# Value products of the later attention runs on 64x64 quarters, in two PSUM banks, with a VectorE add

## The chip, the cores and the metric

The kernel runs on one core of one Trainium2 chip. The metric is device time in microseconds (us). The core has a matrix engine (TensorE, PE in the profile; PEld is its weight load), VectorE (DVE), ScalarE (ACT), GpSimd (POOL) and SyncE (SP), which start from their own instruction lists and wait for each other by semaphores, and DMA queues. Matrix products leave their sums in PSUM, a memory of eight banks of 128 partitions by 512 float32 values.

## The reference, cut to what matters

Three stages follow one another: attention with a window of 128 keys, a feed-forward layer with ReLU, and a gated layer that mixes over the sequence.

```python
scores = scale * np.matmul(q, k.transpose(0, 1, 3, 2))      # B, H, S, D = 4, 8, 576, 64
...
mask = (rel >= 0) & (rel < window)                           # window = 128
scores = np.where(mask, scores + bias[None], -1000000000.0)
...
attn = attn / (np.sum(attn, axis=-1, keepdims=True) + 1e-09)
return np.matmul(attn, v).astype(np.float32)
...
ch = np.maximum(xn @ w_ch1, 0.0) @ w_ch2                     # 512 -> 2048 -> 512, on layer-normed rows
return (x + ch).astype(np.float32)
...
h = x @ w_in                                                 # 512 -> 1024, then a tanh-GELU
u, v = (h[..., :d_ff // 2], h[..., d_ff // 2:])
...
v_s = np.einsum('ts,bsd->btd', w_sg, v_n) + b_sg[None, :, None]
return (x + (u * v_s) @ w_out).astype(np.float32)
```

## The kernel before

Two phases follow each other on the core. `phase1` does attention and the feed-forward layer, the second phase the gated layer.

Attention is cut into 40 runs, numbered n = 0 to 39. Runs 0 to 31 hold two blocks of 128 queries of one pair of heads; their order is batch, half of the sequence (`i0` = 0 or 2), pair of heads, so that four first-half runs (`i0` = 0) and four second-half runs (`i0` = 2) alternate. Runs 32 to 39 are "tails": the last 64 queries of two pairs of heads. A block of queries is a unit; there are 72.

For each run PE makes the scores (`quarters`, L465, L451 for the tails), on tiles of 64x64 of its array. The other engines turn scores into probabilities `t`; PE transposes `t` (`transposed`, L593) into the PSUM bank `tps`; DVE, ACT and POOL copy the transposes, masked, into `m` (L551, L554, L474); PE multiplies `m` by the values (`values`, L633) into columns 0 to 255 of the bank `ob`, and ACT copies that into `x` (L588, L585 for the tails). Partitions 0 to 63 of `ob` are one head, 64 to 127 the other, and columns are queries. A value product takes up to 128 keys by 64 columns of the array (a form 128x64); its passes are three, over the key blocks `i0` - 1, `i0` and `i0` + 1 with 128, 256 and 128 query columns, where a first-half run has only the last two. A tail takes 128 keys and then 64 keys for each pair.

From `KB` = 13 on, PE does attention in bursts (`burst`): the scores of run n + 1, the values of run n - 1 and the transposes of run n, one after the other, without anything between. There are 27 bursts, and the values of run 39 follow alone.

Between the bursts PE does the feed-forward products: L796 (first matrix, into `ps_h`) and L807 (second, into `acc`), each as three products of split operands, twelve matmuls of 128x256 to a half-step. ACT makes the ReLU (L735), DVE the rest of the split (`hl`, L737), and DVE and POOL add the result to `x` (L746, L750). Per group of rows a mean is needed before: POOL sums `x` over its four parts (`sum`, L659 and L661) and PE multiplies that by a matrix of ones (L664); DVE subtracts it (`xc`, L668).

The order on each engine is set at build time by a planner (`Sched`): pieces of work are `Op`s with an engine, an assumed duration, a due time and what they need, and the planner lists them. The durations assumed for bursts (`dur` in `burst`) and for the other pieces shape that order only. Ahead of the first burst the planner fills PE's gaps with matmuls on `ob[:, 256:512]` whose result nobody reads (L853).

Of the kernel before, what the change touches and what calls it, by code (L numbers as in the profile page):

```python
# [11 lines left out]
ACTF = mybir.ActivationFunctionType  # L12
ALU = mybir.AluOpType
# [51 lines left out]
KB = 13  # L65
# [167 lines left out]
def phase1(tc, nc, a, x2d, cst, p2):  # L233
# [37 lines left out]
    ps_s = tc.alloc_tile_pool(name="ps_s", bufs=1, space=PSUM)  # L271
    both = ps_s.tile([128, 2, 2, 256], F32, name="s")
    xt = {}

# [211 lines left out]
    def unit(e):  # L486
# [43 lines left out]
        e.t = t  # L530
        tp = tps[:, un % 2]
        if n >= KB:
# [48 lines left out]
        if sl:  # L581
            xt[x] = xp.tile([128, 4, 256], F32, tag="x", name="x")
        x, p = xt[x], s.p
        if tail:
            act.activation(out=x[:, p:p + 2, s.b * 64:s.b * 64 + 64],  # L585
                           in_=s.O[:, 0:128].rearrange("p (y r) -> p y r", y=2), func=ACTF.Copy)
        else:
            act.activation(out=x[:, p, :], in_=s.O, func=ACTF.Copy)  # L588
        yield Op(None, 0, 0, token=("ev", n))

    def transposed(e):
        for h in range(2):
            pe.transpose(tps[:, e.un % 2, h], e.t[:, h], ident)  # L593

    def burst(s):
# [5 lines left out]
        if after:  # L601
            nd += [("lq", n + 1), ("lk", n + 1)]
            sl.append(("s", 1, ("cp", n + 1)))
        dur = 430 + 140 * len(s.units) + (530 if runs[n - 1].tail else 820 if runs[n - 1].i0 else 600)
        if after:
# [7 lines left out]
        for z in [("A1", n + 1), ("C", n - 1)] + [("T", e.un) for e in s.units]:  # L613
            sched.done[z] = sched.free["PE"] + HOPP

    def values(s):

        s.O = ob[:, 0:256]
        if s.tail:
# [219 lines left out]
    def warm():  # L839

        z = np_.tile([128, 256], F32, tag="rstd", name="zero", bufs=3).bitcast(BF16)
        dve.memset(z, 0.0)
        ps = ps_a.tile([128, 2, 256], F32, tag="a0", name="warm").rearrange("p a b -> p (a b)")
        for n in range(NWARM):
            pe.matmul(ps, z[:, 0:128], z, start=True, stop=True)
        sched.free["PE"] = PE0
        yield Op(None, 0, 0, need=["al"])
        while ("w", 23) not in sched.done:
            yield Op("PE", 213, 10 ** 9)
            if ("w", 23) in sched.done:  # L850
                return
            for x in range(2):
                pe.matmul(ob[:, 256:512], dist[:, 0], dist[:, 0:2], start=True, stop=True, skip_group_check=True)  # L853
            yield Op(None, FILL, 10 ** 9)
# [459 lines left out]
```

## Time and profile before

| | |
|---|---|
| runs of the kernel before | 744.79, 746.72 and 746.82 us, median 746.72 |
| the profiled execution | 746.11 us, of which the span of the trace is 744.4 us |
| PE busy | 728.3 us, 98% of the span |
| DVE, ACT, POOL busy | 454.8, 309.6 and 245.5 us |
| granted clock of TensorE, as a mean | 0.995 of full speed |

The span is the time from the first to the last instruction in the trace; 1.7 us of the execution lie around it. Busy time says how long an engine worked on something; an engine that shows idle time gives with it what released it. The chain that ended last follows the work back from the end, at each step to what released it. A window table gives busy times by stretch, so that a stretch in which PE has no gap is told from one in which it waits.

### The profile page before, as it was taken

How to read it: one execution, taken by the hardware profiler on the slowest of the kernel's cores; microseconds unless marked ns; L12 is line 12 of the kernel's file. 1: busy time of each engine (PE TensorE's matmuls, PEld its weight loads, DVE VectorE, ACT ScalarE, POOL GpSimd, SP SyncE). 2: the span in 40 equal slices, each digit the busy share in tenths (PEclk: the TensorE clock that was granted, in tenths of full speed). 3: DMA queues.
4: the chain of work that ended last, by engine and by line, in shares of the span. 5: the costliest groups of instructions: out<-in, count | busy, mean ns of one | idle time of the engine just before them, and what ended most of it. 6: DMA issues, size and time to landing. Idle time of an engine off the chain costs nothing.

```text
span 744.4 us, 16207 instructions
## 1 busy us (share of the span) xinstructions
PE 728.3 (98%) x6442; PEld 687.8 (92%) x6442; DVE 454.8 (61%) x1173; ACT 309.6 (42%) x794; POOL 245.5 (33%) x295
## 2 busy tenths in 40 slices
PE   6989999999999999999999999999999999999998
PEld 3568999999999999999998999999999999999997
DVE  6899989888562642633533344938585646647632
ACT  5887664444342422422423433323454334243410
POOL 1444250243421411411412222314738307326220
PEclk9999999999999999999999999999999999999999
DMA  9564532032221110111111223423340150160002
GB/s 309 155 206 140 188 103 65 27 92 93 75 87 30 54 51 23 48 58 41 43 48 45 72 76 119 130 98 102 110 128 1 48 158 1 49 207 2 1 33 96
DMA packets 51627, 63.44 MB, mean 85 GB/s; under 512 B 10336, under 2 KB 38880, under 8 KB 51552
## 3 DMA queue, kind: packets, MB, share of 16 engines
q1 hardware_dynamic: 51552, 62.41, 26.7%
q8 instruction: 51, 0.84, 0.5%
q14 instruction: 24, 0.20, 0.1%
HBM read 52.96 MB, written 9.44 MB: 84 GB/s over the span
## 4 chain that ended last, share of the span: by engine, by line
PE 86%; DVE 7%; ACT 4%; POOL 1%; issue 1%; DMA 0%; DVEq 0%; ACTq 0%; SPq 0%
PE acc L807 25%; PE ps_h L796 24%; PE ps_s L1157 8%; PE ps_o L1184 7%; PE ps_v L1061 5%; PE ps_u L1141 5%; PE o L633 4%; PE tps L593 3%; PE s L465 2%; ACT t L516 1%; DVE sc L94 1%; DVE sc L97 1%; ACT t L480 1%; PE s L451 1%; POOL vnl L1051 0%
## 5 line engine op out<-in xcount | busy, mean ns | idle before, releaser
L737 DVE SCALAR_TENSOR_TENSOR hl<-ps_h,hh 128x512 fp32r<-128x512 f32 x72 | 49.7, 690 | 115.0 <-ACT hh L735 114.6
L807 PE MATMUL acc<-hh,w2h 128*128 128x256 f32 x576 | 93.8, 285 | 0.0
L796 PE MATMUL ps_h<-xh,w1h 128*128 128x256 f32 x576 | 91.8, 281 | 0.0
L735 ACT ACTIVATE hh<-ps_h 128x512 fp32r<-128x512 f32 x72 | 42.9, 595 | 114.8 <-PE ps_h L796 114.4
L796 PE MATMUL ps_h<-xh,w1l 128*128 128x256 f32 x576 | 89.8, 278 | 0.0
L796 PE MATMUL ps_h<-xl,w1h 128*128 128x256 f32 x576 | 89.8, 278 | 0.0
L807 PE MATMUL acc<-hh,w2l 128*128 128x256 f32 x576 | 89.6, 278 | 0.0
L807 PE MATMUL acc<-hl,w2h 128*128 128x256 f32 x576 | 89.5, 278 | 0.0
L474 POOL TENSOR_SCALAR_AFFINE_SELECT m<-m 128x256 f32<-128x256 f32 (+1 forms) x85 | 38.6, 455 | 146.1 <-ACT m L554 143.5
L796 PEld LDWEIGHTS ps_h<-xh,w1h 128*128 128x128 f32 x576 | 76.9, 188 | 1.1 <-issue 1.1
L807 PEld LDWEIGHTS acc<-hh,w2h 128*128 128x128 f32 x576 | 77.5, 189 | 0.4
L796 PEld LDWEIGHTS ps_h<-xh,w1l 128*128 128x128 f32 x576 | 76.9, 188 | 0.0
L796 PEld LDWEIGHTS ps_h<-xl,w1h 128*128 128x128 f32 x576 | 76.9, 188 | 0.0
L807 PEld LDWEIGHTS acc<-hh,w2l 128*128 128x128 f32 x576 | 76.8, 188 | 0.0
L807 PEld LDWEIGHTS acc<-hl,w2h 128*128 128x128 f32 x576 | 76.6, 188 | 0.0
L516 ACT ACTIVATE t<-t,sm 128x128 f32<-128x128 f32 x144 | 56.2, 392 | 23.3 <-DVE sm L510 22.8
L524 POOL TENSOR_TENSOR t<-t,sm 128x256 f32<-128x256 f32 x46 | 28.7, 625 | 63.2 <-DVE sm L520 32.9
L1051 POOL TENSOR_TENSOR gl<-gt,gh 128x576 fp32r<-128x576 f32 x16 | 23.4, 1465 | 49.2 <-ACT gh L1050 45.9
L85 ACT ACTIVATE sc<-st 128x512 f32<-128x512 f32 (+1 forms) x52 | 30.6, 600 | 21.3 <-DMA st<-in_w 6.8
L1095 ACT ACTIVATE ge<-ge 128x512 f32<-128x512 f32 (+1 forms) x34 | 22.4, 658 | 36.0 <-DVE ge L1094 36.0
L551 DVE TENSOR_TENSOR m<-tps,munf 128x256 f32<-128x256 f32 x43 | 16.9, 420 | 33.4 <-PE tps L593 32.8
L593 PE MATMUL tps<-ident,t 128*128 128x128 f32 x144 | 28.5, 299 | 8.1 <-POOL t L524 3.7
(160 smaller groups left out, 1587.4 us busy)
## 6 DMA issues: line engine op xcount, KB each, us to landing
st<-in_w SPq DMA_DIRECT2D x24, 512.0 KB, 4.3
x2d<-x SPq DMA_DIRECT2D x18, 256.0 KB, 2.0
out<-xr SPq DMA_DIRECT2D x15, 288.0 KB, 2.1
st<-in_w SPq DMA_DIRECT2D x16, 256.0 KB, 2.7
st<-in_wi SPq DMA_DIRECT2D x8, 512.0 KB, 4.0
st<-x2d SPq DMA_DIRECT2D x8, 512.0 KB, 5.0
xr<-x2d SPq DMA_DIRECT2D x8, 512.0 KB, 7.4
rq<-in_q SPq DMA_DIRECT2D x28, 128.0 KB, 2.7
```

What stands on the lines that cost most here:

```text
L85: self.nc.scalar.activation(out=self.x, in_=self.wh.bitcast(F32), func=ACTF.Abs)
L474: pool.affine_select(out=out, in_=in_, pattern=pat, compare_op=ALU.is_ge, fill=0.0, base=-1 if up else 0, channel_multiplier=1 if up else -1)
L516: act.activation(out=t[:, h], in_=t[:, h], func=ACTF.Exp, bias=st[:, h:h + 1], scale=-1.0, accum_out=sums[:, h, 0:1])
L593: pe.transpose(tps[:, e.un % 2, h], e.t[:, h], ident)
L735: act.activation(out=h, in_=ps, func=ACTF.Relu)
L737: dve.scalar_tensor_tensor(out=l, in0=ps, scalar=0.0, in1=h.bitcast(F32), op0=ALU.max, op1=ALU.subtract)
L796: pe.matmul(ps[:, half], w[:, kc, f], m[:, kc], start=kc == 0 and x == 0, stop=kc == 3 and x == 2)
L807: pe.matmul(accs[half][:, d], w[:, f, ds], m[:, k], start=fi and d == 0 and k == 0 and x == 0, stop=la and k == 1 and x == 2, skip_group_c ...
L1061: self.nc.tensor.matmul(ps[:, cs], xs[s][:, kc, c0:c0 + 128], self.wv[m][:, kc, cs], start=kc == 0 and x == 0 and z == 0, stop=kc == 3 and ...
L1141: pe.matmul(ps[:, c], wu[s][:, kc, ds], self.x[m][:, kc, c], start=kc == 0 and x == 0, stop=kc == 3 and x == 2)
L1157: pe.matmul(ps[:, c], l, r[:, c], start=n == 0, stop=n == len(mm) - 1)
L1184: pe.matmul(ps[:, c], wo[s][:, kc, ds], gated[b][m][:, kc, c], start=n == 0, stop=n == 11)
```

## The change

The runs from 12 on (`KB` - 1) take a new function `quartered`. A product of up to 128 keys by 64 columns becomes two of 64 keys by 64 columns on two different halves of the array's rows: keys 0 to 63 of each block add up in columns 0 to 255 of `ob`, keys 64 to 127 in the same columns of `tps`. The window leaves some query columns of a half without any key; those columns are left out of the product. In a second-half run the first half of the keys has 64 + 192 + 128 columns and the second half 128 + 192 + 64, where the 128-key product had 128 + 256 + 128 = 512. In a first-half run they are 320 and 256 (before 384), in a tail 256 and 128 (before 256, in four steps of 64).

ACT copies `ob` into `x` as before, and DVE then adds the sums in `tps` to `x` (new line, `dve.tensor_tensor`). In first-half runs columns 0 to 63 of the second sums are never written and the add leaves them out. Over 28 runs there are 12 adds of 128x256, 8 of 128x192 and 8 of 128x2x64. The sum on POOL, and so the mean, now needs the add.

Since both banks hold value sums in columns 0 to 255, the transposes from run 13 on go to columns 256 to 511 (`spot`): even units into `ob`, odd ones into `tps`. The planner's assumed durations follow. The filling matmuls end with the first scores of a burst. The lines of the changed program are later by 1 up to the scores (L465 is L466), by 13 at the transposes (L606) and by 39 from the values on (L796 is L835, L659 is L698); the quartered values are L650.

```diff
@@ -270,6 +270,7 @@
     ob = ps_o.tile([128, 512], F32, name="o")
     ps_s = tc.alloc_tile_pool(name="ps_s", bufs=1, space=PSUM)
     both = ps_s.tile([128, 2, 2, 256], F32, name="s")
+    pair = ob, tps.rearrange("p a b c -> p (a b c)")
     xt = {}
 
     def by(o):
@@ -528,7 +529,7 @@
                 scaled(o.eng, t[:, h], t[:, h], st[:, 6 + h:7 + h])
 
         e.t = t
-        tp = tps[:, un % 2]
+        tp = spot(e)
         if n >= KB:
             yield Op(None, 0, pri, need=[("T", un)])
         else:
@@ -581,16 +582,28 @@
         if sl:
             xt[x] = xp.tile([128, 4, 256], F32, tag="x", name="x")
         x, p = xt[x], s.p
+        y = x[:, p, :]
+        os = [z[:, 0:256] for z in pair]
         if tail:
-            act.activation(out=x[:, p:p + 2, s.b * 64:s.b * 64 + 64],
-                           in_=s.O[:, 0:128].rearrange("p (y r) -> p y r", y=2), func=ACTF.Copy)
-        else:
-            act.activation(out=x[:, p, :], in_=s.O, func=ACTF.Copy)
+            y = x[:, p:p + 2, s.b * 64:s.b * 64 + 64]
+            os = [z[:, 0:128].rearrange("p (y r) -> p y r", y=2) for z in pair]
+        act.activation(out=y, in_=os[0], func=ACTF.Copy)
+        if n >= KB - 1:
+            yield Op("DVE", 205 if tail else 340, pri + OC)
+            cut = 64 if i == 1 else 0
+            y, o = (y, os[1]) if tail else (y[:, cut:], os[1][:, cut:])
+            dve.tensor_tensor(out=y, in0=y, in1=o, op=ALU.add)
         yield Op(None, 0, 0, token=("ev", n))
+
+    def spot(e):
+
+        if e.run.n < KB:
+            return tps[:, e.un % 2]
+        return pair[e.un % 2][:, 256:512].rearrange("p (h c) -> p h c", h=2)
 
     def transposed(e):
         for h in range(2):
-            pe.transpose(tps[:, e.un % 2, h], e.t[:, h], ident)
+            pe.transpose(spot(e)[:, h], e.t[:, h], ident)
 
     def burst(s):
         n = s.n
@@ -601,7 +614,7 @@
         if after:
             nd += [("lq", n + 1), ("lk", n + 1)]
             sl.append(("s", 1, ("cp", n + 1)))
-        dur = 430 + 140 * len(s.units) + (530 if runs[n - 1].tail else 820 if runs[n - 1].i0 else 600)
+        dur = 290 + 140 * len(s.units) + (480 if runs[n - 1].tail else 640 if runs[n - 1].i0 else 530)
         if after:
             dur += 530 if after.tail else 850 if after.i0 else 700
         yield Op("PE", dur, (after or s).tau, need=nd, slots=sl)
@@ -613,8 +626,34 @@
         for z in [("A1", n + 1), ("C", n - 1)] + [("T", e.un) for e in s.units]:
             sched.done[z] = sched.free["PE"] + HOPP
 
+    def quartered(s):
+
+
+        a0, a1 = slice(0, 64), slice(64, 128)
+        if s.tail:
+            mm = [[(g, 2 * z, 3, 64 * z, 64 * z, 64) for z in range(2)] for g in (a0, a1)]
+            mm[0] += [(a0, 2 * z + 1, 4, 64 * z, 64 * z, 64) for z in range(2)]
+        else:
+            mm = [[], []]
+            if s.i0:
+                mm[0].append((a0, s.i0 - 1, s.i0 - 1, 0, 0, 64))
+                mm[1].append((a1, s.i0 - 1, s.i0 - 1, 0, 0, 128))
+            mm[0] += [(a0, s.i0, s.i0, 0, 0, 192), (a0, s.i0 + 1, s.i0 + 1, 128, 0, 128)]
+            mm[1] += [(a1, s.i0, s.i0, 64, 64, 192), (a1, s.i0 + 1, s.i0 + 1, 192, 64, 64)]
+        for x in range(len(mm[0])):
+            for g in range(2):
+                if x >= len(mm[g]):
+                    continue
+                k, j, m, oc, mc, w = mm[g][x]
+                for h in range(2):
+                    v = s.v[j // 2][k, j % 2, h, :] if s.tail else s.v[0][k, j - s.k0, h, :]
+                    pe.matmul(pair[g][64 * h:64 * h + 64, oc:oc + w], v, s.M[m][k, h, mc:mc + w], start=x == 0,
+                              stop=x == len(mm[g]) - 1, skip_group_check=True)
+
     def values(s):
 
+        if s.n >= KB - 1:
+            return quartered(s)
         s.O = ob[:, 0:256]
         if s.tail:
             mm = [(128, 2 * z, 3, 64 * z, 64 * z, 64) for z in range(2)]
@@ -845,9 +884,9 @@
             pe.matmul(ps, z[:, 0:128], z, start=True, stop=True)
         sched.free["PE"] = PE0
         yield Op(None, 0, 0, need=["al"])
-        while ("w", 23) not in sched.done:
+        while ("A1", KB) not in sched.done:
             yield Op("PE", 213, 10 ** 9)
-            if ("w", 23) in sched.done:
+            if ("A1", KB) in sched.done:
                 return
             for x in range(2):
                 pe.matmul(ob[:, 256:512], dist[:, 0], dist[:, 0:2], start=True, stop=True, skip_group_check=True)
```

On PE the change shows in the bursts. This is the one with the scores of a first-half run and the values of a second-half run (`o` is `ob`). Before:

```order
L465 MATMUL s<-rk,rq 64x192 x4
L633 MATMUL o<-m,rv 64x128 [waits DMAHW5_49]
L633 MATMUL o<-m,rv 64x128
L633 MATMUL o<-m,rv 64x256 [waits Pool_49]
L633 MATMUL o<-m,rv 64x256
L633 MATMUL o<-m,rv 64x128 [waits Pool_49]
L633 MATMUL o<-m,rv 64x128
L593 MATMUL tps<-ident,t 128x128 [waits Pool_49]
L593 MATMUL tps<-ident,t 128x128
L593 MATMUL tps<-ident,t 128x128 [waits Activation_49] x2
```

Now, on PE in the same burst:

```order
L466 MATMUL s<-rk,rq 64x192 x4
L650 MATMUL o<-m,rv 64x64 [waits DMAHW5_49]
L650 MATMUL o<-m,rv 64x64
L650 MATMUL tps<-m,rv 64x128 x2
L650 MATMUL o<-m,rv 64x192 [waits Pool_49]
L650 MATMUL o<-m,rv 64x192
L650 MATMUL tps<-m,rv 64x192 x2
L650 MATMUL o<-m,rv 64x128 [waits Pool_49]
L650 MATMUL o<-m,rv 64x128
L650 MATMUL tps<-m,rv 64x64 x2
L606 MATMUL o<-ident,t 128x128 [waits Pool_49]
L606 MATMUL o<-ident,t 128x128
```

Six value products became twelve with fewer columns in each bank, and the first two transposes go to `o`; PE waits for the same engines as before.

On DVE, behind the same burst, the copies, the mask and the softmax of the next scores follow. Before:

```order
L737 SCALAR_TENSOR_TENSOR hl<-ps_h,hh 128x512 [waits Activation_49]
L551 TENSOR_TENSOR m<-tps,munf 128x2x128 [waits PE_49]
L500 COPY_PREDICATED s<-mask,mh 128x2x128
L498 COPY_PREDICATED s<-mask,s 128x2x128 [waits DVE_49]
L510 ISA t,sm_121<-s,dist 128x128 [waits DVE_49]
```

Now, on DVE at the same place:

```order
L776 SCALAR_TENSOR_TENSOR hl<-ps_h,hh 128x512 [waits Activation_49]
L552 TENSOR_TENSOR m<-o,munf 128x2x128 [waits Activation_49]
L501 COPY_PREDICATED s<-mask,mh 128x2x128
L595 TENSOR_TENSOR x<-x,tps 128x192 [waits DMAHW3_49,DMAHW4_49,Activation_49,Pool_49]
L511 ISA t,sm_121<-s,dist 128x128 [waits DVE_49]
```

The product `m` waits for ACT (its copy out of the same bank) where it waited for PE, and the add stands ahead of the softmax.

On POOL the sum for a group's mean is the place where the add is waited for, here for the group of runs 20 to 23. Before:

```order
L659 TENSOR_TENSOR sum<-x 128x512 [waits Activation_49]
L474 AFFINE_SELECT m<-m 128x2x128 [waits Activation_49]
L661 TENSOR_TENSOR sum<-sum 128x256 [waits Pool_49]
L474 AFFINE_SELECT m<-m 128x256 [waits PE_49,Pool_49]
L524 TENSOR_TENSOR t<-t,sm_121 128x256 [waits DVE_49,PE_49,Activation_49]
```

Now, on POOL at the same place:

```order
L475 AFFINE_SELECT m<-m 128x2x128 [waits Activation_49]
L698 TENSOR_TENSOR sum<-x 128x512 [waits DVE_49]
L475 AFFINE_SELECT m<-m 128x256 [waits PE_49,Pool_49]
L700 TENSOR_TENSOR sum<-sum 128x256 [waits Pool_49]
L525 TENSOR_TENSOR t<-t,sm_121 128x256 [waits DVE_49,PE_49,Activation_49]
```

The sum waits for DVE where it waited for ACT, and one of the mask selects moved ahead of it.

## Rows read from the trace of the kernel before

**Rows 1.** Page: busy time of each engine (share of the span), then the chain's shares.

```profile
PE 728.3 (98%) x6442; PEld 687.8 (92%) x6442; DVE 454.8 (61%) x1173; ACT 309.6 (42%) x794; POOL 245.5 (33%) x295
...
PE 86%; DVE 7%; ACT 4%; POOL 1%; issue 1%; DMA 0%; DVEq 0%; ACTq 0%; SPq 0%
```

**Rows 2.** Windows: stretch, length, busy PE, PEld, DVE, ACT, POOL, granted clock, DMA share.

```profile
128.00:200.00 72.00, 72.00 (x672) 69.02 (x672) 57.42 (x159) 33.76 (x96) 27.32 (x36) 1.00 0.22 68
200.00:300.00 100.00, 100.00 (x951) 94.22 (x951) 45.26 (x151) 32.05 (x102) 22.45 (x36) 1.00 0.18 53
300.00:400.00 100.00, 100.00 (x934) 94.33 (x934) 44.86 (x152) 33.43 (x105) 22.60 (x38) 1.00 0.16 45
400.00:455.00 55.00, 55.00 (x571) 50.87 (x568) 18.47 (x67) 20.46 (x65) 15.65 (x27) 1.00 0.27 76
455.00:600.00 145.00, 144.54 (x1208) 144.25 (x1208) 96.05 (x153) 58.24 (x97) 64.04 (x51) 1.00 0.29 94
```

**Rows 3.** Timeline (start, length, xrecords), PE: burst, first-half scores, second-half values.

```profile
165.78 0.77 PE L465 MATMUL s<-rk,rq 64*64 64x64 f32 x16
166.48 1.09 PE L633 MATMUL o<-m,rv 128*64 128x128 f32 x12
167.50 0.66 PE L593 MATMUL tps<-ident,t 128*128 128x128 f32 x4
167.91 0.72 PE L807 MATMUL acc<-hh,w2h 128*128 128x256 f32 x4
```

**Rows 4.** Timeline, PE: burst with second-half scores and first-half values.

```profile
227.61 0.88 PE L465 MATMUL s<-rk,rq 64*64 64x192 f32 x16
228.42 0.87 PE L633 MATMUL o<-m,rv 128*64 128x256 f32 x8
229.23 0.66 PE L593 MATMUL tps<-ident,t 128*128 128x128 f32 x4
```

**Rows 5.** Timeline, PE: a tails' burst, and the last values, alone.

```profile
421.21 0.56 PE L451 MATMUL s<-rk,rq 64*64 64x192 f32 x8
421.70 0.83 PE L633 MATMUL o<-m,rv 128*64 128x64 f32 x16
422.46 0.44 PE L593 MATMUL tps<-ident,t 128*128 128x128 f32 x2
...
451.80 0.83 PE L633 MATMUL o<-m,rv 128*64 128x64 f32 x16
452.56 0.61 PE L807 MATMUL acc<-hh,w2h 128*128 128x256 f32 x3
```

**Rows 6.** Timeline: from a burst's transposes to a group's mean (runs 20 to 23).

```profile
297.25 0.66 PE L593 MATMUL tps<-ident,t 128*128 128x128 f32 x4
...
297.36 0.38 ACT L588 ACTIVATE x<-o 128x256 f32<-128x256 f32 x1 [2.43 <-PE o L633]
...
297.83 1.29 POOL L659 TENSOR_TENSOR sum<-x 128x512 f32<-128x512 f32 x1 [8.24 <-ACT x L588]
...
297.94 0.42 DVE L551 TENSOR_TENSOR m<-tps,munf 128x256 f32<-128x256 f32 x1 [2.29 <-PE tps L593]
...
299.07 0.60 POOL L474 TENSOR_SCALAR_AFFINE_SELECT m<-m 128x256 f32<-128x256 f32 x1
...
299.44 0.43 DVE L498 COPY_PREDICATED s<-mask,s 128x256 f32<-128x256 uint8 x1
...
299.64 0.74 POOL L661 TENSOR_TENSOR sum<-sum 128x256 f32<-128x256 f32 x1
...
301.85 0.59 PE L664 MATMUL ps_ln<-sum,ones 128*128 128x256 f32 x2
```

**Rows 7.** Timeline: where DVE frees `acc` shortly before PE writes it.

```profile
193.07 0.67 DVE L746 TENSOR_TENSOR et<-acc,rstd 128x512 f32<-128x512 f32 x1
...
194.25 0.63 PE L807 MATMUL acc<-hh,w2h 128*128 128x256 f32 x4
```

## The prediction

> **What bounds the kernel now.** I read the page's busy times and its chain first. PE is busy for 98% of the span and carries 86% of the chain, DVE 61% and 7% [rows 1]. Shares over the whole span say nothing of one stretch, so the windows come next. The change touches the time from the first burst, at 128 us, to the last values, at 452 us. In the four stretches from 128 to 455 us PE is busy for every microsecond, at the full granted clock (1.00, the 2.4 GHz level), while DVE works 57.42, 45.26, 44.86 and 18.47 us [rows 2]. The reader should see there that PE waits for nobody: what is taken out of PE's own list comes out of the time, and what is put on other engines costs nothing until PE has to wait for it. After 455 us PE is still busy for 144.54 of 145 us, so an earlier start is passed on.
>
> Then I read the bursts in PE's timeline, each as the distance from one section's first matmul to the next section's first, since the lengths of single records overlap. With first-half scores and second-half values: scores 0.70 us, values 1.02, transposes 0.41 [rows 3]. With second-half scores and first-half values: 0.81, 0.81 and 0.41 [rows 4]. With tails: 0.49, 0.76, 0.19 [rows 5]. The records count two per product, so twelve records are six products.
>
> Columns explain these lengths. The four quarters of the array work at once in the scores, and the fullest has 320 columns in the first-half runs, 384 in the second-half ones, 192 in the tails. 64 columns more take 0.11 us, that is about 1.67 ns for a column, and 0.16 to 0.17 us are left over each time (0.81 - 384 x 1.67 ns = 0.17; 0.49 - 0.32 = 0.17). The values obey the same law with 512 and 384 columns: 1.02 - 0.855 = 0.165 and 0.81 - 0.64 = 0.17. The tails' values are the row that tells what the constant is: 0.76 - 256 x 1.67 ns = 0.33, twice the constant, and they alone change their tile inside the section (128 rows, then 64). So I take 0.165 us as the price of a change of tile shape, not of a product: eight products in the tails leave no further price per product.
>
> **The change, part by part.** *Fewer columns.* The fullest quarter of a second-half run falls from 512 to 384 columns, of a first-half run from 384 to 320, and of a tail it stays at 256. *No change of shape.* Scores and values are now both 64x64, so the constant between them goes; the one ahead of the transposes stays. A tail also loses the change inside its section.
>
> - 12 second-half runs: 128 x 1.67 ns + 0.165 = 0.38 us each, 4.6 us
> - 8 first-half runs: 64 x 1.67 ns + 0.165 = 0.27 us each, 2.2 us
> - 6 tails whose values follow scores: 2 x 0.165 = 0.33 us each, 2.0 us
> - the last 2 tails, whose values follow the feed-forward products (as at 451.80 [rows 5]) and still change shape once: 0.165 us each, 0.3 us
>
> That is 9.1 us, all of it on an engine without a gap.
>
> *More products.* 136 more are issued. No row shows twelve products in 0.43 us, as a tail now has; the nearest is eight in 0.43 [rows 5], 54 ns each. From below the price is nothing (the law above holds without one), from above it is that those 54 ns are a floor: the second-half runs then just keep their 0.64 us (12 x 53 ns), the tails take 0.65, and 8 x 0.22 = 1.7 us go. I take nothing, since the eight in the tails' row fit the columns exactly, and keep 1.7 for the range.
>
> The Trainium skill speaks against the change here: "TensorEngine Tiling (Array Packing)", section Instruction Overhead, gives every matmul on TRN2 about 60 cycles of its own. At 2.4 GHz that is 25 ns, an estimate of 3.4 us for 136 products, and the sum would be 5.7 us instead of 9.1. The tails' row, with no price left beside the columns, does not bear it out.
>
> *28 adds on DVE.* None is in the trace; the nearest, a product of two 128x256 operands with one in PSUM, took 0.42 us [rows 6]. At most 28 x 0.42 = 11.8 us, on an engine with 166 busy of 327 us [rows 2]. Two additions `x` + `et` also come from POOL to DVE, each about as long as the `et` of the same size, 0.67 us [rows 7]. As load this costs nothing; if DVE had no room it would be the whole 11.8.
>
> *New waits.* The order lists put none on PE. But ACT's copy of `ob` now also waits for the two transposes into `ob`, DVE's product for that copy, the add for these, and POOL's sum for the add; PE waits for the sum at each group's mean, five times in the stretch. The rows at 297 us have the chain [rows 6]. ACT's copy began at 297.36, the sum at 297.83, the second sum ended at 300.38, and PE took it at 301.85: 1.47 us to spare. Now: half of the transposes (0.2) and the 0.28 us that DVE needed behind them put ACT's copy at 297.74; it ends at 298.12; product 0.42, mask 0.43 and add 0.42 follow on DVE; the sum starts about 299.4, 1.6 us later. So PE waits some 0.1 us there, and 0.5 us in five such places. Below: nothing, where the add comes ahead of the mask or the group has more to spare. Above: the sum starts only after the mask of 299.44 has ended and the add has followed, at 300.3, so 2.5 us late, 1.0 us a place and 5 us in all.
>
> The tightest wait on another engine is at 194 us: DVE ended `et` at 193.74, PE wrote `acc` at 194.25 [rows 7], 0.5 us to spare. An add of 0.42 and a product that starts 0.3 us later can use up 0.7 of it, 0.2 us of waiting. PE's other waits on attention come only with the next burst.
>
> The Trainium skill, "PSUM — Partial Sum Buffer", section "PSUM bank collisions raise a hardware error", has engines kept apart by bank (and quarter of the partitions) even where their columns differ. That is why the copy, the product and the transposes of one bank now follow each other. Were columns enough, ACT's copy would start where it did and the 0.5 us of give-back would shrink to about 0.1.
>
> *The rest* (planner durations, filling matmuls, transposes in other columns): the order on PE outside the values is the same up to the last tails, whose bursts come two half-steps earlier. No price.
>
> Sum: 746.1 of the profiled execution (span 744.4 and 1.7 around it) - 9.1 + 0.5 + 0.2 = 737.7. The profiled execution lies 0.6 under the median of 746.7; a saving of 8.4 from the median would be 738.3. I say 737.9.
>
> **The rivals.** *New waits become the bound.* For it: four engines now stand in one chain between burst and mean, and 1.47 us is all there was. Against it: the five places are few and the last group's values come earlier. It gives back 1.5 to 5 us instead of 0.7: 738.7 to 742.2, at its middle 740.3.
>
> *A price per product.* If each product takes 54 ns at least, whatever its columns, the tails give back 1.7 us and the time is 739.4. For it: no row is as dense as the new tails. Against it: the tails' row, where eight fit the columns. The figure of the Trainium skill ("TensorEngine Tiling (Array Packing)", Instruction Overhead) would make it 741.1.
>
> *It doesn't do what it says: the constant stays.* If the 0.165 us belongs to the start of any section that reads new data, and not to the shape, 26 sections between scores and values keep it: 4.3 us, 742.2. Against it: the tails' second constant stands inside a section.
>
> *Slower: the two halves of the rows take turns.* If the two halves of the array's rows run one after the other, a second-half run has 768 columns in a row (+256, 0.43 - 0.165 = +0.26 us), a first-half run 576 (+0.16), a tail 384 (0.21 - 0.33 = -0.12; the last two +0.05): 3.1 + 1.3 - 0.7 + 0.1 = +3.8 us, and with the waits 750.6. It decides where the halves overlap by less than some 30% (9.1 against 12.9). Against it: the scores' rows, where quarters on both halves of the rows, into two banks, keep the law of the fullest quarter [rows 3, 4].
>
> **How the numbers follow.** Forecast, 736 to 739.5: 0.68. Waits: 0.14. Price per product: 0.09. Constant stays: 0.05. Slower: 0.03. Left for none of these, around no change: 0.01. The forecast and the waits up to 741.5 hold more than 8 in 10; below, adds that are free and a run like the fastest of before (744.8) reach to 735. So 735 to 741.5. About 0.3%, 2.2 us, is what a measurement of this kernel can tell from no change: faster than 744.5 are all cases but the last two and an unlikely heap of waits, 0.94; the same 0.03; slower 0.03.
>
> **What would show it.** In the changed kernel's PE timeline: values 0.64 us in a second-half run, 0.53 in a first-half one, 0.43 in a tail (0.60 in the last two), with scores and transposes at 0.70, 0.81, 0.49, 0.41 as before. Values near 0.81 in second-half runs would be the constant, 0.65 in tails the floor per product, 1.28 in second-half runs the halves in turn. PE's idle time from 128 to 455 us, now none, should be under 1 us and stand ahead of the means and of `acc` writes; several microseconds there would be the waits. PE idle time behind 455 us that was not there before would make the prediction wrong in a way that I gave no price.

## The result, and the profile after

The changed kernel takes 738.5 us (median of four runs, 738.03 to 739.1) against 746.6 for the kernel before: a ratio of 0.9897, with an interval of 0.988 to 0.9915. That is 8.1 us less; the forecast was 737.9, in a range of 735 to 741.5. The profiled execution took 738.73 us, with a span of 737.0.

The page of the changed kernel, busy time by engine and the shares of the chain, answers to [rows 1]:

```profile
span 737.0 us, 16770 instructions
...
PE 720.1 (98%) x6714; PEld 691.0 (94%) x6714; DVE 460.3 (62%) x1200; ACT 309.1 (42%) x795; POOL 249.2 (34%) x296
...
PE 83%; DVE 7%; ACT 5%; issue 2%; POOL 1%; DMA 1%; SPq 0%; DVEq 0%; ACTq 0%
```

PE lost 8.2 us of busy time and has 272 more records (136 products, two each); DVE and POOL gained 5.5 and 3.7 us. The windows of the changed kernel (columns as in [rows 2], the last values now end at 441 us):

```profile
128.00:200.00 72.00, 72.00 (x748) 70.96 (x749) 58.25 (x162) 35.03 (x99) 26.96 (x36) 1.00 0.22 68
200.00:300.00 100.00, 100.00 (x1040) 97.84 (x1031) 49.38 (x171) 34.52 (x113) 24.26 (x38) 1.00 0.18 54
300.00:400.00 100.00, 100.00 (x1048) 97.63 (x1048) 46.89 (x154) 33.80 (x105) 23.98 (x38) 1.00 0.17 48
400.00:446.00 46.00, 46.00 (x570) 44.40 (x570) 20.69 (x70) 16.72 (x53) 14.33 (x25) 1.00 0.34 100
446.00:600.00 154.00, 152.56 (x1268) 152.08 (x1267) 96.70 (x155) 60.79 (x101) 63.84 (x50) 1.00 0.29 96
```

PE is still busy for every microsecond of the bursts, at the full granted clock: none of the new waits reached it there. Behind them it now idles 1.44 us up to 600 us, where 0.46 us were idle in [rows 2].

Three bursts in PE's timeline, with the scores' first row, the values' first row and the transposes, answer to [rows 3 to 5]: first-half scores with second-half values, second-half scores with first-half values, a tail.

```profile
165.29 0.77 PE L466 MATMUL s<-rk,rq 64*64 64x64 f32 x16
165.79 0.22 PE L650 MATMUL o<-m,rv 64*64 64x64 f32 x1
...
166.66 0.44 PE L606 MATMUL o<-ident,t 128*128 128x128 f32 x2
...
167.07 0.72 PE L846 MATMUL acc<-hh,w2h 128*128 128x256 f32 x4
```

```profile
225.64 0.88 PE L466 MATMUL s<-rk,rq 64*64 64x192 f32 x16
226.34 0.32 PE L650 MATMUL o<-m,rv 64*64 64x192 f32 x1
...
226.99 0.44 PE L606 MATMUL o<-ident,t 128*128 128x128 f32 x2
```

```profile
399.94 0.56 PE L452 MATMUL s<-rk,rq 64*64 64x192 f32 x8
400.31 0.22 PE L650 MATMUL o<-m,rv 64*64 64x64 f32 x1
...
400.88 0.44 PE L606 MATMUL tps<-ident,t 128*128 128x128 f32 x2
```

The scores look shorter than forecast (0.50 instead of 0.70 at 165.29). That is where the section now ends in the records and not a gain: with the same tile shape on both sides, the first value products start on a quarter that is done while a fuller one still works on scores. So scores and values have to be read together, from the first score to the first transpose. The table shows each kind of values behind one kind of scores; behind other scores both times shift alike (second-half values behind second-half scores: 1.83 and 1.47), and the last column counts all runs of the kind:

| scores and values together | before | after | less | forecast | runs |
|---|---|---|---|---|---|
| second-half values (behind first-half scores) | 1.72 | 1.36 | 0.36 | 0.38 | 12 |
| first-half values (behind second-half scores) | 1.61 | 1.35 | 0.26 | 0.27 | 8 |
| tails behind scores | 1.25 | 0.94 | 0.30 | 0.33 | 6 |
| last two tails, values alone | 0.76 | 0.61 | 0.15 | 0.165 | 2 |

With the third digit (0.362, 0.264, 0.303, 0.149) that is 4.3 + 2.1 + 1.8 + 0.3 = 8.6 us, where the forecast had 9.1. The differences of a kind agree within 2 ns, whatever scores stand ahead.

PE's waits from 441 us to the end, in the changed kernel and then in the kernel before from 452 us. `ps_s` is a bank of the second phase, for the product that mixes over the sequence; `vt` is one operand of that product, which ACT and POOL split into two parts:

```profile
PE ps_s L1196 <- POOL vt L1090: 1.1, 1, 1.1
PE acc L846 <- DVE hl L776: 0.3, 1, 0.3
```

```profile
PE ps_s L1157 <- POOL vt L1051: 0.5, 1, 0.5
```

So the span's 7.4 us are 8.6 less in the bursts, 0.9 to 1.0 more in these two places, and 0.24 because the first burst began later (128.20 instead of 127.96 us). Idle time is the lower reckoning: by the starts of PE's products the two places lose 1.3 us against the kernel before, and some 0.3 us come back outside the bursts, for which no run shows a cause.

Much of the spread between runs lies ahead of the first burst. In the profiled runs of all kernels here that burst comes between 125.6 us (both moves together, below), where the granted clock is 1.00 from the start, and 130.1 us (halves in order), where it is 0.91, 0.92 and 0.83 in the first three stretches of 20 us; from the first burst to 730 us it is 1.00 in all of them. So a difference of a microsecond between two totals has to be checked against the traces. Counted from the first burst to the end of the span, the kernel before takes 616.4 us and the changed kernel 608.8, which is 7.6 less.

### The profile page after: what moved, and what is told of

Its sections match the earlier page's. It is cut to its first block, busy times and chain, and to the rows that moved or that the text cites. A ratio compares the mean times of both kernels' runs of the same rounds, so it can differ in the third digit from the quotient of the medians.

```text
span 737.0 us, 16770 instructions
## 1 busy us (share of the span) xinstructions
PE 720.1 (98%) x6714; PEld 691.0 (94%) x6714; DVE 460.3 (62%) x1200; ACT 309.1 (42%) x795; POOL 249.2 (34%) x296
## 4 chain that ended last, share of the span: by engine, by line
PE 83%; DVE 7%; ACT 5%; issue 2%; POOL 1%; DMA 1%; SPq 0%; DVEq 0%; ACTq 0%
PE ps_h L835 24%; PE acc L846 24%; PE ps_s L1196 8%; PE ps_o L1223 7%; PE ps_v L1100 5%; PE ps_u L1180 5%; PE s L466 2%; PE tps L606 1%; PE o L650 1%; ACT t L517 1%; PE o L606 1%; DVE sc L94 1%; DMA bb<-in_bsg 1%; PE tps L650 1%; DVE sc L97 1%
## 5 line engine op out<-in xcount | busy, mean ns | idle before, releaser
L835 PE MATMUL ps_h<-xh,w1h 128*128 128x256 f32 x576 | 92.1, 282 | 0.0
L835 PE MATMUL ps_h<-xh,w1l 128*128 128x256 f32 x576 | 89.7, 278 | 0.0
L835 PE MATMUL ps_h<-xl,w1h 128*128 128x256 f32 x576 | 89.7, 278 | 0.0
L475 POOL TENSOR_SCALAR_AFFINE_SELECT m<-m 128x256 f32<-128x256 f32 (+1 forms) x87 | 41.7, 481 | 136.6 <-ACT m L555 121.8
L835 PEld LDWEIGHTS ps_h<-xh,w1h 128*128 128x128 f32 x576 | 77.2, 189 | 1.3 <-issue 1.2
L835 PEld LDWEIGHTS ps_h<-xh,w1l 128*128 128x128 f32 x576 | 76.8, 188 | 0.0
L835 PEld LDWEIGHTS ps_h<-xl,w1h 128*128 128x128 f32 x576 | 76.8, 188 | 0.0
L590 ACT ACTIVATE x<-o 128x256 f32<-128x256 f32 (+1 forms) x40 | 14.3, 358 | 58.3 <-PE o L606 46.1
L97 DVE SCALAR_TENSOR_TENSOR sc<-st,sc 128x512 int32<-128x512 int32 (+1 forms) x52 | 34.9, 678 | 0.1
```

Source lines behind the costliest of these rows:

```text
L97: dve.scalar_tensor_tensor(out=xi, in0=self.wl, scalar=29, in1=xi, op0=ALU.logical_shift_right, op1=ALU.bitwise_or)
L475: pool.affine_select(out=out, in_=in_, pattern=pat, compare_op=ALU.is_ge, fill=0.0, base=-1 if up else 0, channel_multiplier=1 if up else -1)
L835: pe.matmul(ps[:, half], w[:, kc, f], m[:, kc], start=kc == 0 and x == 0, stop=kc == 3 and x == 2)
```

## What the saving is made of: four experiments in the bursts

The theory was that a section lasts as long as its fullest quarter, at 1.67 ns a column, plus 0.165 us for each change of tile shape, with no price per product; the rivals were a price per product, a constant that belongs to any section, and halves that take turns.

**All columns.** The products over columns that no key reaches are put back.

```diff
-                mm[0].append((a0, s.i0 - 1, s.i0 - 1, 0, 0, 64))
+                mm[0].append((a0, s.i0 - 1, s.i0 - 1, 0, 0, 128))
...
-            mm[0] += [(a0, s.i0, s.i0, 0, 0, 192), (a0, s.i0 + 1, s.i0 + 1, 128, 0, 128)]
-            mm[1] += [(a1, s.i0, s.i0, 64, 64, 192), (a1, s.i0 + 1, s.i0 + 1, 192, 64, 64)]
+            mm[0] += [(a0, s.i0, s.i0, 0, 0, 256), (a0, s.i0 + 1, s.i0 + 1, 128, 0, 128)]
+            mm[1] += [(a1, s.i0, s.i0, 0, 0, 256), (a1, s.i0 + 1, s.i0 + 1, 128, 0, 128)]
...
-            cut = 64 if i == 1 else 0
+            cut = 0
```

> The changed kernel with all query columns kept in both halves (second-half runs 128 + 256 + 128 in each bank, first-half runs 256 + 128; the columns that the window leaves without keys are zero, and the add takes all 256). Products, tile shapes and banks stay. Theory (the fullest quarter's columns set the length): scores and values together get 128 x 1.67 ns = 0.21 us longer in 12 second-half runs and 64 x 1.67 ns = 0.11 us in 8 first-half runs, tails unchanged; 3.4 us in all, 738.5 -> 741.9. Rival (the saving came from the tile shape alone, columns don't count): 738.5.

Measured 742.0 us (740.3 to 743.1), 3.5 more than the changed kernel. Its burst at 166 us, timeline of PE:

```profile
166.01 0.77 PE L466 MATMUL s<-rk,rq 64*64 64x64 f32 x16
...
167.58 0.44 PE L606 MATMUL o<-ident,t 128*128 128x128 f32 x2
```

1.57 us instead of 1.36: 0.21 more, as expected, and 0.11 more in first-half runs. The term of the columns is right, and the rival that gives it all to the shape is out.

**Transposes between scores and values**, so that a burst changes shape four times and not twice.

```diff
-        values(runs[n - 1])
         for e in s.units:
             transposed(e)
+        values(runs[n - 1])
```

> The changed kernel with the transposes of a burst issued between its scores and its values, nothing else moved on PE. Scores and values are 64x64 tiles, transposes and feed-forward products 128x128, so a burst changes shape four times instead of twice. Theory (0.165 us for each change of shape): 2 x 0.165 us in each of 26 bursts with scores, 8.6 us, 747.1. Rival (the constant belongs to the start of any section, whatever its shape): as many sections as before, 738.5, and the values after the transposes no longer than now.

Measured 748.1 us (745.8 to 749.8). Timeline of PE:

```profile
167.52 0.78 PE L466 MATMUL s<-rk,rq 64*64 64x64 f32 x16
168.22 0.44 PE L606 MATMUL o<-ident,t 128*128 128x128 f32 x2
...
168.81 0.27 PE L650 MATMUL o<-m,rv 64*64 64x64 f32 x2
...
169.63 0.74 PE L846 MATMUL acc<-hh,w2h 128*128 128x256 f32 x4
```

From scores to feed-forward products 2.11 us, where the changed kernel has 167.07 - 165.29 = 1.78: 0.33 more with the same products, and 0.33 in the tails' and the first-half bursts too. That is two changes of 0.165 us. The constant belongs to the shape. (The median is 1.0 us above what 26 such bursts make; in the profiled run the first burst began 1.5 us later than in the changed kernel's, and from there to the end it takes 8.55 us more.)

**Twice the products**, each of half the columns.

```diff
-            for g in range(2):
+            for y, g in ((0, 0), (0, 1), (1, 0), (1, 1)):
...
                 k, j, m, oc, mc, w = mm[g][x]
+                w //= 2
+                oc, mc = oc + y * w, mc + y * w
...
-                    pe.matmul(pair[g][64 * h:64 * h + 64, oc:oc + w], v, s.M[m][k, h, mc:mc + w], start=x == 0,
-                              stop=x == len(mm[g]) - 1, skip_group_check=True)
+                    pe.matmul(pair[g][64 * h:64 * h + 64, oc:oc + w], v, s.M[m][k, h, mc:mc + w], start=x + y == 0,
+                              stop=x == len(mm[g]) - 1 and y == 1, skip_group_check=True)
```

> The changed kernel with every value product cut into two of half the columns: 24 in a second-half run or a tail, 16 in a first-half run, same columns. Theory (no price per product beside the columns): 738.5. Rival, a floor of 54 ns per product: 24 x 54 ns = 1.30 us instead of 0.64 in second-half runs, 0.86 instead of 0.53 in first-half runs, 1.30 instead of 0.43 in tails; 12 x 0.66 + 8 x 0.33 + 8 x 0.87 = 17.5 us, 756. A price between shows first in the tails, where 24 products have 0.43 us, 18 ns each, then in the second-half runs (27 ns) and last in the first-half runs (33 ns). The Trainium skill, "TensorEngine Tiling (Array Packing)", Instruction Overhead, gives about 60 cycles a matmul, an estimate of 25 ns at 2.4 GHz; as a floor that would be 0.60 us in the tails alone, 1.4 us in all, 739.9.

Measured 745.2 us (743.8 to 746.2). A tail in its timeline of PE:

```profile
402.71 0.56 PE L452 MATMUL s<-rk,rq 64*64 64x192 f32 x8
403.09 0.19 PE L652 MATMUL o<-m,rv 64*64 64x32 f32 x1
...
404.10 0.44 PE L606 MATMUL tps<-ident,t 128*128 128x128 f32 x2
```

Scores and values take 1.38 us (0.94 in the changed kernel). With the scores' own 0.486 as in [rows 5], 24 products take 0.90 us, 37 ns each, whatever their 32 columns would need (18 ns). In second-half runs 24 products take 0.79 (1.599 - 0.811 for the scores), 33 ns each, where columns would make it 0.64. In first-half runs 16 take 0.55, 35 ns each, just above their 0.53 us of columns. So there is a floor, of 33 to 37 ns a product; why it differs between the kinds is not shown. The theory of no price falls, and so does the rival's 54 ns. The floor reaches the changed kernel only in the tails: 12 x 37 = 0.45 us is what they took (0.944 - 0.486 = 0.46), not the 0.43 of their columns. The Trainium skill ("TensorEngine Tiling (Array Packing)", Instruction Overhead) has about 60 cycles a matmul, at 2.4 GHz an estimate of 25 ns, and says that a free dimension of 1 takes as long as one of 60. The runs show a floor of that kind with another figure: 33 to 37 ns for a product, which is two records, so 16 to 19 ns a record.

The bursts make 12 x 0.13 + 8 x 0.02 + 8 x 0.44 = 5.2 of the 6.7 us that this kernel is longer. In its trace the stretches between the bursts are longer too, 2.75 us in all: four feed-forward products mostly take 0.47 us there from start to start, in the changed kernel 0.45 to 0.46, at the same granted clock of 1.00. What slows them is not shown.

**The halves one after the other in the list.**

```diff
-        for x in range(len(mm[0])):
-            for g in range(2):
+        for g in range(2):
+            for x in range(len(mm[0])):
```

> The changed kernel with all products of the first half of the keys issued before those of the second half, same products otherwise. Theory (a product starts in its place in PE's list, when its quarter is free, and the halves overlap only if they are issued in turns): in a second-half run the second half starts when the first half's last product does, at 256 columns, and ends at 640 instead of 384, +0.43 us; first-half runs end at 384 instead of 320, +0.11; tails at 320 instead of 256, +0.11. 12 x 0.43 + 16 x 0.11 = 6.8 us: 745.3. Rival (each quarter takes its own products whatever the order): 738.5. Rival (the halves take turns already): 738.5 too, with values of 1.28 us in the changed kernel's second-half runs.

Measured 741.25 us (740.4 to 742.1), between the two expectations. Timeline of PE, second-half values:

```profile
167.54 0.77 PE L466 MATMUL s<-rk,rq 64*64 64x64 f32 x16
168.03 0.55 PE L650 MATMUL o<-m,rv 64*64 64x64 f32 x6
168.27 0.33 PE L650 MATMUL tps<-m,rv 64*64 64x128 f32 x2
168.31 0.44 PE L650 MATMUL o<-m,rv 64*64 64x192 f32 x2
...
168.59 0.38 PE L650 MATMUL o<-m,rv 64*64 64x128 f32 x3
...
169.07 0.33 PE L606 MATMUL o<-ident,t 128*128 128x128 f32 x1
```

The products into `tps` stand behind all six into `o` in PE's list, yet they start at 168.27, before products into `o` that start at 168.31 and 168.59. So a product that waits for its quarter does not hold up the next one for another quarter. The six products into `o` take 0.24 us to be handed out (40 ns each, near the floor above), and by about that much the second half starts late. A second-half run loses 0.17 us, a tail 0.06, a first-half run nothing, where I had 0.43, 0.11 and 0.11; 12 x 0.17 + 8 x 0.06 = 2.5 us, and 2.75 were measured. The bursts carry this reading and not the total, since the first burst of the profiled run alone began 1.9 us later than in the changed kernel. My picture of products that start strictly in list order was wrong; taking turns in the list is worth some 2.6 us, not 6.8.

## Where the rest went: the tails, the adds, the planner

**Tails as before**, without halves or add.

```diff
-        if s.n >= KB - 1:
+        if s.n >= KB - 1 and not s.tail:
             return quartered(s)
...
-        if n >= KB - 1:
+        if n >= KB - 1 and not tail:
             yield Op("DVE", 205 if tail else 340, pri + OC)
```

> The changed kernel with the tails' values in the form of before (128 and 64 keys by 64 columns, into one bank, without an add). Theory (a tail gains by the two changes of shape alone, measured as 0.30 us in six tails and 0.15 in the last two): 2.1 us more, 740.6. Rival (a tail's gain is eaten by its twelve products, or by the adds behind them): 738.5 or less.

Measured 739.6 us (738.8 to 740.4). The tails' bursts are back at 1.25 us, 2.1 us lost, but the order of the other engines changed with it and the wait for `vt` is 0.5 us and not 1.1, with none for `hl`. 738.5 + 2.1 - 0.9 = 739.7. The tails' term is real; that the total shows only half of it has to do with the late waits, below.

**No add.**

```diff
-            dve.tensor_tensor(out=y, in0=y, in1=o, op=ALU.add)
```

> The changed kernel without the 28 adds on VectorE (so x lacks the sums of the second half of the keys, and POOL's sum waits for ACT again). Theory (the adds lie beside PE's work and no wait of PE before the last values comes from them): bursts unchanged, no idle time of PE from 128 to 441 us, 738.5 within 0.5 us. Rival (the adds load VectorE on the path): up to 28 x 0.42 = 11.8 us less, 727 to 737.

Measured 738.4 us (737.0 to 739.8), the same as the changed kernel, with the same bursts. The 28 adds, 0.29 to 0.42 us each and 10.0 us together, cost PE nothing.

**The planner's assumed durations as before.**

```diff
-        dur = 290 + 140 * len(s.units) + (480 if runs[n - 1].tail else 640 if runs[n - 1].i0 else 530)
+        dur = 430 + 140 * len(s.units) + (530 if runs[n - 1].tail else 820 if runs[n - 1].i0 else 600)
```

> The changed kernel with the durations that the planner assumes for a burst as they were before (430, 530, 820 and 600 instead of 290, 480, 640 and 530). The products are the same; VectorE, POOL and ScalarE get another order in places. Theory (the gain is in the products; the assumed durations only shape an order in which PE waits for nobody): the bursts take as long as in the changed kernel, 738.5 within 1 us. Rival (part of the gain, or of the late waits, comes from the planner's new order): PE idle in the stretch of the bursts, 740 or more, or the late waits gone, 737.5.

Measured 737.8 us (737.4 to 739.6), with bursts as in the changed kernel and the wait for `vt` at 1.2 us. The new order is neither the gain nor the wait for `vt`. The wait of 0.3 us for `hl` does not occur here.

## The late waits

In the second phase DVE halves a bias, `bb`, that comes by DMA, and stands in its list until it is there. Its waits and its late additions in the changed kernel, with POOL's splits of a weight (`wsl`):

```profile
505.70 0.46 DVE L1007 TENSOR_SCALAR bb<-bb 128x576 f32<-128x576 f32 x1 [4.23 <-DMA bb<-in_bsg]
...
520.34 7.45 POOL L1090 TENSOR_TENSOR wsl<-st,wsh 128x576 fp32r<-128x576 f32 x5
...
524.51 0.69 DVE L785 TENSOR_TENSOR et<-acc,rstd 128x512 f32<-128x512 f32 x1 [0.72 <-PE acc L846]
525.12 3.21 DVE L789 TENSOR_TENSOR x<-x,et 128x512 f32<-128x512 f32 x2
```

And in the kernel before:

```profile
512.73 0.46 DVE L968 TENSOR_SCALAR bb<-bb 128x576 f32<-128x576 f32 x1 [2.75 <-DMA bb<-in_bsg]
...
527.40 6.99 POOL L1051 TENSOR_TENSOR wsl<-st,wsh 128x576 fp32r<-128x576 f32 x5
...
532.42 0.69 DVE L746 TENSOR_TENSOR et<-acc,rstd 128x512 f32<-128x512 f32 x1 [0.72 <-PE acc L807]
533.03 2.51 DVE L750 TENSOR_TENSOR x<-x,et 128x512 f32<-128x512 f32 x2
```

Measured from the last `et`, `bb` is used 0.9 us later than before (18.8 instead of 19.7 us ahead of it), what hangs on DVE and POOL behind it moves by as much, POOL's splits run on beside the last two additions for longer (2.7 us instead of 1.4), and these take 3.21 us and not 2.51. What follows, the chain over `vt` to PE, is late by that 0.7. The wait for `hl` is less clear: it occurs here and with the transposes between (0.2 us), but in none of the other kernels with a late `bb`, and no experiment isolates it. The DMA itself was slower. Its window in the changed kernel (rates in 40 equal slices, then packets by kind, then time to landing):

```profile
GB/s 0 0 0 140 94 234 164 211 211 234 328 445 351 375 421 492 351 398 398 398 383 415 354 366 343 241 221 41 24 23 23 26 26 26 13 14 0 0 0 0
...
q8 instruction: 1, 0.02, 0.9%
...
bb<-in_bsg SPq DMA_DIRECT2D x1, 288.0 KB, 6.1
```

Before, `bb` landed sooner:

```profile
bb<-in_bsg SPq DMA_DIRECT2D x1, 288.0 KB, 4.7
```

The tail of the transfer runs at 23 to 26 GB/s, about a sixteenth of the some 400 before it, as if one of the 16 engines were behind; the trace does not say which engine took what. The packet of the kind "instruction" in the same window is a piece of 16 KB of PE's list. There are 53 of them in the changed kernel and 51 before, and by the packets' records one starts in the middle of the transfers now (22.7 us ahead of the last `et`), and before it started 0.3 us ahead of their end (20.4 us, where they ended at 20.1), not after them as the next expectation has it. The next two experiments take this link from either end: one moves the fetch, the other takes the wait for `bb` off DVE.

**The fetch moved**: the filling matmuls in halves, 72 instructions more in PE's list and no work more.

```diff
-            for x in range(2):
-                pe.matmul(ob[:, 256:512], dist[:, 0], dist[:, 0:2], start=True, stop=True, skip_group_check=True)
+            for x in range(4):
+                pe.matmul(ob[:, 256:384], dist[:, 0], dist[:, 1], start=True, stop=True, skip_group_check=True)
```

> The changed kernel with each of the 36 filling matmuls before the first burst issued as two of half the columns: 72 instructions more in PE's list, no work more. PE's instructions are fetched by DMA in pieces of 16 KB, every 12 to 15 us; in the changed kernel such a fetch starts 22.7 us before the last et, in the middle of the transfers of wo, x2d and bb (which end 19.2 us before it); in the kernel before the fetch started after them (20.35 us before et) and they ended 20.1 us before it. Theory (the fetch on one DMA ring holds up bb's last packets by 0.8 us, and that is what PE pays for in the second phase): with 72 of 256 instructions of a piece more, the fetch comes some 4 us earlier, ahead of the transfers; bb is used 0.8 us earlier and PE's late waits go from 1.4 to 0.5 us, 737.5. Rival (the fetch's place doesn't matter): bb and the waits stay, 738.5.

Measured 736.85 us (735.8 to 737.2). The same window and the wait of PE:

```profile
GB/s 0 0 0 85 311 282 0 0 169 226 282 169 339 452 395 452 452 424 424 311 424 424 367 452 424 373 408 366 445 397 213 209 6 0 0 0 0 0 0 0
...
bb<-in_bsg SPq DMA_DIRECT2D x1, 288.0 KB, 4.6
```

```profile
PE ps_s L1196 <- POOL vt L1090: 0.3, 1, 0.3
```

The fetch has left the window, the slow tail is gone, `bb` lands in 4.6 us, the wait of 1.1 us is 0.3 and that for `hl` is gone. Of the 2.2 us between the two profiled runs, 1.4 lie behind the start of the first burst. All kernels that keep `bb` on DVE fall in the same two groups (us ahead of the last `et`; a fetch at 28 or more is ahead of the transfers):

| kernel | fetch starts | transfers end | PE waits for vt |
|---|---|---|---|
| before | 20.4 | 20.1 | 0.5 |
| twice the products | 20.0 | 19.9 | 0.5 |
| tails as before | 31.3 | 19.9 | 0.5 |
| filling in halves | 28.2 | 20.2 | 0.3 |
| after | 22.7 | 19.2 | 1.1 |
| all columns | 22.8 | 19.2 | 1.2 |
| halves in order | 22.7 | 19.2 | 1.2 |
| transposes between | 21.3 | 19.2 | 1.1 |
| no add | 22.8 | 19.4 | 1.0 |
| planner as before | 22.7 | 19.2 | 1.2 |

**The wait moved**: `bb` and `g2` are halved on POOL.

```diff
-            self.nc.vector.tensor_scalar(x, x, 0.5, None, ALU.mult)
+            self.nc.gpsimd.tensor_scalar(x, x, 0.5, None, ALU.mult)
```

> The changed kernel with the halving of the bias bb and of g2 (two small instructions at the start of the second phase that wait for their DMA) on POOL instead of VectorE. Theory (VectorE stands 4.2 us behind the DMA of bb at 501 us; its late work makes PE wait 0.3 us at 511 us, and, by way of POOL's splits of the weights, which then run beside VectorE's last additions, 0.7 us more at 552 us): both waits shrink to what they were, 1.0 us less, 737.5. Rival (these waits have another cause): 738.5, and PE still waits 1.1 us for vt.

Measured 736.28 us (736.17 to 736.29), ratio 0.9852 (0.9828 to 0.9876) to the kernel before. PE waits nowhere from 128 us to the end. Of the 2.4 us between the two profiled runs, 0.6 lie ahead of the first burst (127.57 against 128.20 us). By the starts of PE's products 0.6 us are gained at the place of the wait for `hl` and 1.2 at that for `vt`: 1.8, where the idle time was 1.4. The fetch is still inside the transfers (22.1 us), but nothing that PE needs stands behind them:

```profile
515.92 6.98 POOL L1090 TENSOR_TENSOR wsl<-st,wsh 128x576 fp32r<-128x576 f32 x5
...
523.29 0.69 DVE L785 TENSOR_TENSOR et<-acc,rstd 128x512 f32<-128x512 f32 x1 [0.72 <-PE acc L846]
523.90 1.28 DVE L789 TENSOR_TENSOR x<-x,et 128x512 f32<-128x512 f32 x2
```

The splits end at 522.90, before the additions begin, and these take 1.28 us for the two instead of 3.21. The Trainium skill, "SBUF — State Buffer", section "SBUF: two separate sides", says that POOL and a VectorE instruction with two inputs in SBUF share a port that one of them holds for a whole instruction; these additions, 1.28, 2.51 and 3.21 us with none, some and more of the splits beside them, agree. That it is this port which slows them, no run here shows apart.

**The same move in the kernel before** (the diff above on the old code), and **both moves together** in the changed kernel (this diff and that of the fetch):

> The kernel before with only the halving of bb and g2 on POOL. Its one late wait of PE, for vt, is 0.46 us in the trace. Theory (the late waits were 0.5 us before the change and the change made 0.9 more of them): 0.5 us less than the kernel before, 746.1 to 746.2, and no wait for vt. Rival (the move to POOL is worth 2 us by itself, whatever the change did): 744.5.

> The changed kernel with bb and g2 halved on POOL and with each filling matmul as two halves. Theory (PE waits for nobody any more once bb is on POOL, so the place of the fetch has nothing left to give): as with bb on POOL alone, 736.3. Rival (the two gains add up): 734.7.

The first measured 745.6 us (ratio 0.9982, 0.9972 to 0.9993), 1.3 less than the kernel before beside it, where 0.5 was expected; its wait for `vt` is gone, and the interval of 0.5 to 2.1 us has the expected gain at its edge; in the traces the products behind that wait gain 0.6 to 0.7 us. The second measured 736.6 us (734.3 to 737.9), as the move to POOL alone: they do not add up, as expected. From the first burst to the end both profiled runs take 607.0 us.

## Why the prediction was right, step by step

- **Columns.** Right in size: 0.21 and 0.11 us came back when the columns did.
- **Change of shape.** Right: 0.33 us for two more of them in each burst. The tails, which gain by it alone, gave 2.1 us of the 2.3 that I had put down.
- **No price per product.** Wrong as a statement, small in effect. The eight products of [rows 5] fit their columns at 54 ns each because the floor lies at 33 to 37 ns, not because there is none; the tails went below it and lost 0.03 us each. The other 0.01 to 0.02 us that second-half bursts lack against the forecast have no experiment. Together this is 9.1 against 8.6.
- **The chain to the means.** The mechanism was right and cost nothing. I expected the sum to start 1.6 us later and PE to wait some 0.1 us. The rows of the changed kernel for [rows 6]:

```profile
293.60 0.44 PE L606 MATMUL o<-ident,t 128*128 128x128 f32 x2
...
294.07 0.38 ACT L590 ACTIVATE x<-o 128x256 f32<-128x256 f32 x1 [2.48 <-PE o L606]
...
295.42 0.41 DVE L595 TENSOR_TENSOR x<-x,tps 128x256 f32<-128x256 f32 x1
...
295.91 1.29 POOL L698 TENSOR_TENSOR sum<-x 128x512 f32<-128x512 f32 x1 [0.69 <-DVE x L595]
...
297.53 0.74 POOL L700 TENSOR_TENSOR sum<-sum 128x256 f32<-128x256 f32 x1
...
298.34 0.69 PE L703 MATMUL ps_ln<-sum,ones 128*128 128x256 f32 x2
```

  The sum starts 2.31 us after the transposes, where it was 0.58 [rows 6]: 1.7 later. It ends at 298.27, and PE takes it at 298.34: of the 1.47 us to spare, at most 0.07 are left, so that PE did not wait is a close call here. At 194 us [rows 7] PE did not wait either. So the 0.7 us that I took back in the bursts were 0.
- **Behind the bursts.** I named idle time there as what would make the prediction wrong in a way without a price. It came, 0.9 to 1.0 us of it, and so the total is right by two errors of half a microsecond to a microsecond against each other: 9.1 - 0.7 forecast, 8.6 - 1.0 in the trace.

## What to carry to other kernels

In these runs a section with tiles of one shape on all quarters lasted as long as its fullest quarter, to within 0.03 us; count columns per quarter, add one constant for each change of shape, and see that no product falls below the floor of its hand-out (33 to 37 ns here). When an engine without a gap gets shorter, look behind it too: here the place of an instruction fetch shifted with the length of PE's list and went with a microsecond lost in a stretch that nobody had changed, and moving the fetch alone won most of it back. An instruction that waits for a DMA should stand on an engine behind which nothing urgent is queued; moving two such small ones made the changed kernel 2.2 us faster by the medians, 1.8 of it at PE's late waits. And where two totals differ by a microsecond, compare the traces from the same point on: the first burst alone began up to 4.5 us apart in these profiled runs.

## What the runs showed of the hardware that I had not expected

- A product for a busy quarter does not hold up a later one for a free quarter: products into `tps` started 0.32 us ahead of products into `o` that stand before them in the list.
- A fetch of 16 KB of PE's instructions in the middle of three transfers made the last of them land in 6.1 us instead of 4.7, with a tail at 23 to 26 GB/s. That both shared one DMA engine is inferred from that tail and not shown.
- Idle time understates what a wait costs PE: the two waits of the changed kernel, 1.4 us idle, held back the products behind them by 1.8 us.
- The spread of some 4 us between runs of one kernel goes with the granted clock: of the 43 runs of the kernel before beside the experiments, the 13 with 0.995 or more as a mean took 746.0 us on average, the 20 with 0.992 or less 747.6. In the profiled runs what is lost lies in the first 60 us and at the very end; what makes the clock fall there is not shown.
